# Loads of a batch held back until the convolution two batches earlier

## The chip, the core and the metric

The kernel runs on one core of one Trainium2 chip. The metric is the device time of one execution in microseconds (us). All times below are of that kind, or are read from the hardware profile of one execution.

## What is computed

The input x has 8 batches of 4224 rows with 192 columns, in float32. Two stages follow one another. Shortened from the reference:

```python
# stage 1: causal convolution along the rows, 7 taps, one softmaxed tap vector per head
w = softmax(weight)                       # 8 heads x 7 taps; a head is 24 of the 192 columns
y[b, s, h, :] = sum_k w[h, k] * x[b, s + k - 6, h, :]
# stage 2: mixing over the rows of a batch
W_tok = (y @ w_q) @ (y @ w_k).T / 8       # 4224 x 4224 per batch
out = relu(W_tok @ y) @ w_out
```

The kernel never forms W_tok. It uses that (y w_q)(y w_k)^T y is (y w_q) times the small matrix w_k^T (y^T y), so each batch needs the 192x192 Gram matrix y^T y, a 64x192 matrix made from it, and then row by row products.

## The kernel before

**Tiling.** A batch is cut into 35 chunks of 122 rows (NCC = 35). Each chunk is loaded with the 6 rows before it, so that one 128x128 band matrix per head does the convolution of a chunk as one matrix product. Loads go in groups of chunks: batch 0 has four groups (9, 9, 9 and 8 chunks), each later batch has two (18 and 17 chunks). The tile `XW` (line 355) has room for all 8 batches, so no load overwrites anything that is still read.

**Loads** (`gen_load`, lines 535 to 574). A load is issued by POOL with `e.dma_start` on line 565, and converts float32 to bfloat16 on its way. The first group of a batch is two DMAs (chunk 0, which lacks the 6 rows before it, and the other 17), the last group is two as well (16 chunks, and the short last one). That makes 34 DMAs. POOL does nothing else after the start apart from building the identity (line 426), and it issues the loads in the order of the batches. In the kernel before, a load of a later batch needs only the identity, the zeroed end of `XW`, or nothing: POOL may issue it at any time.

**Convolution** (`gen_conv`, lines 636 to 675). For each group there are four matrix operations, one per pair of heads (hp 0 to 3), each of four matmuls (lines 391 and 392) from `XW` and `BAND` into PSUM. An evacuation by ACT or DVE (line 671) writes `Y`, which has two buffers: batch b uses the buffer of batch b-2. Each of the four operations needs the load of its group.

**Later stages.** Of `Y` the kernel makes transposes (lines 691 and 726), the Gram matrix (line 787), the product with w_q (lines 751 and 755), the mixing (lines 878 and 890), a relu (lines 907 and 908) and the product with w_out (lines 935 and 953). The result goes through `out_sb`, four buffers, and out by DMAs that SP issues (line 978). The mixing of batch b runs beside the convolution, transposes and Gram matrix of batch b+1.

**Order.** Every operation is an `Op` with its engines, the operations that it needs, those that it only has to follow (`after`), and a priority `vt` taken from the list `TURNS` by the operation's number. `Planner.plan` (lines 143 to 213) places them one after another at planned times: an operation can be chosen once all that it needs or follows is placed, it is ready when what it needs has ended, and among the ready ones of an engine the lowest `vt` goes first. For a load, the planned landing is the later of its end plus 1500 ns and a fixed figure `lands` (line 573). `Program.place` (lines 232 to 274) then turns each need into a semaphore wait on the engine's own instruction stream, and leaves out those that an earlier wait covers. PE, ACT, DVE, POOL and SP each run their stream in that fixed order.

Of the kernel before, what the change touches and what calls it, by code (L numbers as in the profile page):

```python
# [279 lines left out]
def bass_lightweight_conv__then__hypermixer_token_mlp_kernel(  # L280
# [33 lines left out]
    def groups_of(b):  # L314
        size = 9 if b == 0 else 18
        return [list(range(c, min(c + size, NCC))) for c in range(0, NCC, size)]
# [60 lines left out]
    def add(*a, dma=None, kind=None, **k):  # L377
        op = Op(*a, **k)
        op.dma = dma
        op.kind = kind  # L380
        op.vt = TURNS[len(planner.ops)]
        return planner.add(op)

    def evac_ns(cols, fast=1):
        return {"ACT": 56 + cols / 1.2, "DVE": 62 + cols / (0.96 * fast)}
# [3 lines left out]
    def halves(e, out, lhsT, rhs, **k):  # L389

        e.matmul(out[0:64], lhsT[:, 0:64], rhs, **k)  # L391
        return e.matmul(out[64:128], lhsT[:, 64:128], rhs, **k)  # L392
# [137 lines left out]


    load = {}
    at = [5000.0]

    def gen_load(b, gi):
# [97 lines left out]
    def mm_ns(n, k=1):  # L633
        return k * (n / 2.4 + 2.5)

    def gen_conv(b, gi):
        cs = groups_of(b)[gi]
        n = len(cs)
        c0, yb = cs[0], b % 2
        pairs_in_bank = 2 * n * GRP <= 512  # L640
        nb = 1 if pairs_in_bank else 2
        gap = n * GRP if pairs_in_bank else 512
        for hp in range(H // 2):
            vt = b + c0 / NCC - 0.15 + 0.02 * hp

            def conv(e, op, hp=hp):
                last = None
                for i in range(2):
                    h = 2 * hp + i
                    o = op.bank * 512 + i * gap  # L650
                    last = halves(
                        e,
                        PS[:, o : o + n * GRP],
                        BAND[:, h, :],
                        XW[:, b, c0 : c0 + n, GRP * h : GRP * h + GRP],
                        start=True,
                        stop=True,
                    )
                return last

            ev_needs = [r for r in y_read.get((b - 2, "all"), [])]
            mm = add(
                "PE", conv, mm_ns(n * GRP, 2), needs=[*load[b, gi], *bands, zero_x, zero_x0], after=ev_needs, banks=nb, vt=vt, kind="conv")

            def evac(e, op, hp=hp, mm=mm):
                o = mm.bank * 512
                src = PS[0:CW, o : o + 2 * gap].rearrange("p (t n) -> p t n", t=2)[:, :, 0 : n * GRP]
                src = src.rearrange("p t (c g) -> p t c g", g=GRP)
                dst = Y[0:CW, yb, c0 : c0 + n, 2 * GRP * hp : 2 * GRP * hp + 2 * GRP]
                dst = dst.rearrange("p c (t g) -> p t c g", t=2)  # L670
                return e.copy(dst, src) if op.engine == "ACT" else e.tensor_copy(dst, src)  # L671

            ev = add(both, evac, evac_ns(2 * n * GRP), needs=ev_needs, drains=mm, vt=vt, kind="y")
            for c in cs:
                y_done.setdefault((b, c), []).append(ev)
# [312 lines left out]
    for b in range(B + 1):  # L988
        nxt = []
        if b < B:  # L990
            for gi in range(len(groups_of(b))):
                gen_conv(b, gi)
            for c in range(0, NCC, 8):
                gen_transpose(b, list(range(c, min(c + 8, NCC))))
            evqs = [gen_wq(b, j) for j in range(NSB)]
            grams = []
            step = 6
            for c in range(0, NCC, step):
                cs = list(range(c, min(c + step, NCC)))
                grams += gen_gram(  # L1000
                    b, cs, c == 0, c + step >= NCC, [g_read] if c == 0 and g_read else [], grams[:1]
                )
            evm = gen_mix_weights(b, grams)
            nxt = [(b, j, evm, evqs[j]) for j in range(NSB)]
        for job in later:
            gen_mix(*job)
        later = nxt

    planner.plan()

    program = Program(semaphore)
# [47 lines left out]
```

## Time and profile before

| What | Value |
|---|---|
| median of 3 runs | 177.17 us (176.81, 177.17, 178.93) |
| profiled execution, first to last instruction | 175.7 us, that is 1.5 us under the median |
| PE busy (matmul) | 157.1 us, 89% |
| ACT, DVE busy | 123.5 us, 118.0 us |
| POOL busy | 30.3 us, all of it in the first 53 us |
| bytes moved by the DMA engines | 40.36 MB, mean 230 GB/s |
| loads of x (queue q0) | 36128 packets, 13.61 MB as written |
| stores (most of queue q1) | 44 DMAs, 25.95 MB written to HBM |
| granted TensorE clock, mean | 0.990 |

The profile lists no separate run time for the profiled execution, so its span stands for it, and the 1.5 us are what a run has beyond the span, together with the scatter of the runs.

The page gives the busy time of each engine, then the span in 40 slices of 4.4 us with a digit for the busy share in tenths, then the DMA queues, then the chain of work that ended last. In that chain, "issue" is time in which an engine waited for nothing that the profile shows. Line numbers are those of the kernel.

### The profile page before, as it was taken

What the parts mean: (1) busy time and instruction counts of PE and PEld (TensorE: products, weight loads), DVE (VectorE), ACT (ScalarE), POOL (GpSimd) and SP (SyncE); (2) the same over time, 40 slices, a digit from 0 to 9 for tenths busy, and PEclk for the clock granted to TensorE, in tenths of its full rate; (3) what the DMA queues carried; (4) which work ended last, traced back from release to release, by engine and by line L of the source; (5) the groups of instructions that cost most, each with busy time, mean ns of one, the idle gap of its engine ahead of it and who ended that gap; (6) DMA issues with size and microseconds to landing.
All of it is one profiled execution on the core that took longest, in us unless ns stands there. A gap on an engine that the chain in (4) does not pass through costs nothing.

```text
span 175.7 us, 7099 instructions
## 1 busy us (share of the span) xinstructions
PE 157.1 (89%) x3226; PEld 121.7 (69%) x3226; DVE 118.0 (67%) x216; ACT 123.5 (70%) x206; POOL 30.3 (17%) x39
## 2 busy tenths in 40 slices
PE   0289799888999999899989979999999999999990
PEld 0179666776787787668778766878767777877550
DVE  6556587765766677586787738689688675765740
ACT  3243677597787948668648747888888896698980
POOL 7999452524230000000000000000000000000000
PEclk9999999999999999999999999999999999999995
DMA  3999999999999999999999999067283045987787
GB/s 30 162 189 186 205 191 193 191 196 277 193 279 194 286 309 268 343 250 243 304 264 282 237 194 348 24 244 297 103 343 127 4 175 216 356 347 309 265 303 262
DMA packets 48157, 40.36 MB, mean 230 GB/s; under 512 B 37632, under 2 KB 40960, under 8 KB 48128
## 3 DMA queue, kind: packets, MB, share of 16 engines
q0 software_dynamic: 36128, 13.61, 65.1%
q1 hardware_dynamic: 12000, 26.31, 40.9%
q8 instruction: 25, 0.41, 0.9%
q14 instruction: 4, 0.03, 0.1%
HBM read 27.56 MB, written 25.95 MB: 305 GB/s over the span
## 4 chain that ended last, share of the span: by engine, by line
PE 88%; issue 4%; DVE 3%; ACT 2%
PE ps L391 25%; PE ps L787 14%; PE ps L935 8%; PE ps L392 7%; PE ps L395 6%; PE ps L726 6%; PE ps L878 5%; PE ps L751 4%; PE ps L890 4%; PE ps L755 4%; PE ps L396 3%; ACT rt L907 1%; ACT out_sb L970 1%; DVE band L527 0%; DVE xw L416 0%
## 5 line engine op out<-in xcount | busy, mean ns | idle before, releaser
L970 ACT COPY out_sb<-ps 128x768 f32<-128x768 f32 (+1 forms) x46 | 34.7, 768 | 15.1 <-PE ps L392 11.3
L671 ACT CAST y<-ps 122x816 bf16<-122x816 f32 (+3 forms) x46 | 35.7, 791 | 13.2 <-PE ps L392 12.8
L907 ACT ACTIVATE rt<-ps 128x1024 bf16<-128x1024 f32 (+3 forms) x44 | 34.1, 800 | 6.4 <-PE ps L878 4.5
L787 PE MATMUL ps<-y 122*64 122x192 bf16 (+4 forms) x840 | 33.8, 222 | 2.2 <-issue 2.2
L970 DVE COPY out_sb<-ps 128x768 f32<-128x768 f32 (+1 forms) x26 | 21.6, 840 | 19.7 <-PE ps L392 18.5
L392 PE MATMUL ps<-wol,rt 128*64 128x192 bf16 x264 | 33.9, 255 | 1.0 <-issue 1.0
L787 PEld LDWEIGHTS ps<-y 122*64 122x64 bf16 (+1 forms) x840 | 31.1, 112 | 4.9 <-issue 2.8
L565 POOL DMA_DIRECT2D xw<-in_x_dram x34 | 29.9, 893 | 22.3 <-issue 21.5
L391 PE MATMUL ps<-wol,rt 128*64 128x192 bf16 x264 | 33.7, 255 | 0.0
L391 PE MATMUL ps<-xw,band 128*64 128x432 bf16 (+3 forms) x144 | 31.8, 335 | 1.5 <-DVE band L527 0.9
L392 PE MATMUL ps<-xw,band 128*64 128x432 bf16 (+3 forms) x144 | 32.1, 337 | 1.1 <-issue 1.1
L391 PEld LDWEIGHTS ps<-wol,rt 128*64 128x64 bf16 x264 | 24.1, 138 | 8.1 <-issue 2.0
L908 DVE TENSOR_SCALAR rt<-ps 128x512 bf16<-128x512 f32 (+3 forms) x36 | 23.6, 674 | 8.2 <-PE ps L878 7.6
L671 DVE CAST y<-ps 122x864 bf16<-122x864 f32 (+3 forms) x26 | 23.6, 912 | 8.0 <-PE ps L392 7.5
L698 DVE COPY ytl<-ps 128x976 bf16<-128x976 bf16 (+1 forms) x40 | 23.0, 591 | 3.9 <-PE ps L396 3.3
L392 PEld LDWEIGHTS ps<-wol,rt 128*64 128x64 bf16 x264 | 24.1, 138 | 1.2 <-issue 1.2
L396 PE MATMUL ps<-ident,y 122*64 122x122 bf16 x280 | 21.1, 219 | 0.0
L395 PE MATMUL ps<-ident,y 122*64 122x122 bf16 x280 | 21.0, 219 | 0.0
L935 PE MATMUL ps<-woh,rt 64*128 64x192 bf16 x264 | 20.4, 250 | 0.2 <-ACT rt L907 0.2
L395 PEld LDWEIGHTS ps<-ident,y 122*64 122x64 bf16 x280 | 18.1, 112 | 2.0 <-issue 0.5
L726 PE MATMUL ps<-ident,y 122*64 122x122 bf16 (+1 forms) x344 | 17.1, 220 | 1.3 <-DVE y L671 0.7
L396 PEld LDWEIGHTS ps<-ident,y 122*64 122x64 bf16 x280 | 17.7, 112 | 0.0
(95 smaller groups left out, 218.8 us busy)
## 6 DMA issues: line engine op xcount, KB each, us to landing
out_dram<-out_sb SPq DMA_DIRECT2D x28, 768.0 KB, 5.1
xw<-in_x_dram POOLq DMA_DIRECT2D x7, 816.0 KB, 33.2
xw<-in_x_dram POOLq DMA_DIRECT2D x7, 768.0 KB, 33.7
out_dram<-out_sb SPq DMA_DIRECT2D x8, 384.0 KB, 3.3
xw<-in_x_dram POOLq DMA_DIRECT2D x2, 432.0 KB, 8.3
out_dram<-out_sb SPq DMA_DIRECT2D x8, 96.0 KB, 4.3
xw<-in_x_dram POOLq DMA_DIRECT2D x1, 384.0 KB, 5.2
xw<-in_x_dram POOLq DMA_DIRECT2D x8, 45.8 KB, 25.0
```

The source lines that it names most:

```text
L391: e.matmul(out[0:64], lhsT[:, 0:64], rhs, **k)
L392: return e.matmul(out[64:128], lhsT[:, 64:128], rhs, **k)
L395: e.transpose(out[0:64], in_[:, 0:64], identity)
L396: return e.transpose(out[64:128], in_[:, 64:128], identity)
L565: lambda e, op, part=part: e.dma_start(*part),
L671: return e.copy(dst, src) if op.engine == "ACT" else e.tensor_copy(dst, src)
L726: last = e.transpose(ps[64 * i : 64 * i + HI, o : o + w], Y[0:w, yb, c, LO:D], IDENT[0:w, 0:w])
L787: mm = e.matmul(bank(GB)[p : p + 64, o : o + z - r], Y[0:w, yb, c, r : r + 64], Y[0:w, yb, c, r:z], start=st, stop=end, skip_group_check=True,
L907: return e.activation(dst, src(), AF.Relu)
L908: return e.tensor_scalar(dst, src(), 0.0, None, op0=ALU.max)
L935: last = e.matmul(bank(op.bank + a)[:, o : o + D], RT[64 * a : 64 * a + HI, slot, 2, i:n:nt], WOH[64 * a : 64 * a + HI, :], start=i == q, ...
L970: return e.copy(dst, src) if op.engine == "ACT" else e.tensor_copy(dst, src)
```

## The change

After all operations are made, and before the planner runs, every load of a batch from 2 on gets one more need: a convolution of the batch two before it. A batch from 3 on waits, group by group, for the same group of that batch. Batch 2 waits for groups 0 and 2 of the four groups of batch 0. `conv_of[b, gi]` is overwritten in the loop over the pairs of heads, so it holds the operation of hp 3, whose place in the planner's order need not be the last of the four.

```diff
     load = {}
+    conv_of = {}
     at = [5000.0]
...
-            mm = add(
+            mm = conv_of[b, gi] = add(
                 "PE", conv, mm_ns(n * GRP, 2), needs=[*load[b, gi], *bands, zero_x, zero_x0], after=ev_needs, banks=nb, vt=vt, kind="conv")
...
+    for (b, gi), ops in load.items():
+        if b >= 2:
+            for op in ops:
+                op.needs.append(conv_of[b - 2, gi if b > 2 else 2 * gi])
+
     planner.plan()
```

It touches 24 of the 34 load DMAs, and 12 groups. No operation is added or removed, and no transfer changes its size.

## The prediction, made before the changed kernel ran

> **What bounds the kernel now.** I read the page first (busy times, slices, chain), then the chain in order of time, then POOL's timeline and the DMA views.
>
> ```profile
> PE 157.1 (89%) x3226; PEld 121.7 (69%) x3226; DVE 118.0 (67%) x216; ACT 123.5 (70%) x206; POOL 30.3 (17%) x39
> ...
> PE   0289799888999999899989979999999999999990
> ...
> DMA  3999999999999999999999999067283045987787
> ...
> q0 software_dynamic: 36128, 13.61, 65.1%
> ...
> PE 88%; issue 4%; DVE 3%; ACT 2%
> ```
>
> PE is the bound: 88% of the chain that ended last is its own work. The DMA engines are full from the start to slice 25 (25 x 4.4 = 110 us), and then have room. The loads of x (q0) are what fills them: the trace's last q0 packet starts at 105.66 us. PE's dips (7, 8, 7) lie in the full part; from there to the last slice but one it is at 9 throughout. The stretches say the same:
>
> ```profile
> 92.00:106.00 14.00, 13.01 (x308) 10.77 (x303) 9.15 (x16) 9.03 (x16) 0.00 (x0) 1.00 1.26 244
> 106.00:116.00 10.00, 10.00 (x185) 7.16 (x183) 7.70 (x17) 8.67 (x13) 0.00 (x0) 1.00 0.38 147
> ```
>
> The first pair is the window and its length, the second PE's busy time and count, the last three the granted clock, the DMA share and GB/s. PE loses 1 us in 14 with the loads, nothing in 10 without, at the same clock of 1.00. What it loses there stands in the chain:
>
> ```profile
> 19.20 1.28 issue
> ...
> 32.64 0.50 issue
> ...
> 39.08 1.07 issue
> ...
> 70.06 0.90 issue
> ...
> 89.60 0.59 issue
> ...
> 102.10 0.99 issue
> ```
>
> Six pauses, 5.33 us, and no data is waited for in them. I counted PE's instructions (matmuls and weight loads together) up to each: 448, 960, 1216, 2496, 3264 and 3776, all 192 past a multiple of 256. The instruction queue of the DMA page (q8) has 25 packets of 16384 B, one about every 6 us, 0.9 to 1.0 us each, and each of the six pauses ends 1.4 to 1.5 us after one has landed. So they are waits for PE's next 256 instructions. Until 100.72 us, under the loads, 14 such fetches start, when PE is 43 to 120 instructions short of the block, and 6 come late. The 11 after 104 us start 134 to 264 short, and none is late. One loaded fetch costs 5.33 / 14 = 0.38 us on average.
>
> The Trainium skill, page "Runtime: NRT & Kernel Launch", section "Instruction fetch mechanics", has the same blocks of 16 KiB and 256 instructions, and says that the cost of crossing a block is mostly hidden. The trace agrees on the block and not on the cost, 5.33 us; by that page the third term below would be 0 and the sum 177.2.
>
> Last, POOL, whose issues the change touches:
>
> ```profile
> 2.63 16.51 POOL L565 DMA_DIRECT2D xw<-in_x_dram  x19
> 21.63 2.26 POOL L565 DMA_DIRECT2D xw<-in_x_dram  x3 [2.48 <-issue]
> ...
> 51.29 1.71 POOL L565 DMA_DIRECT2D xw<-in_x_dram  x2 [4.16 <-issue]
> ```
>
> And the landings of the same line (issue to landing):
>
> ```profile
> DMA to landing us min/median/max: 4.1/28.7/53.9
> ```
>
> POOL runs far ahead: 20 issues in the first 19 us, the last at 52.5, and up to 53.9 us pass until a landing. A load waits in its own queue, not for POOL. This decides the case: a load that is issued later loses nothing while an earlier load still keeps the queue busy.
>
> **The change part by part.** (1) The waits. 24 DMA instructions get a need and 12 of them become a wait on POOL. Behind them on POOL stand only later loads, and none of those is let go sooner than the one ahead of it. SP and its stores are not passed or held. PE, ACT and DVE get no instruction. POOL is idle from 53 us on, so the waits themselves cost 0. A load's two issues take about 1.8 us (1.2 and 0.6) and the first q0 packet starts 3.02 - 1.30 = 1.7 us after its issue began.
>
> (2) Landings. The release is the end of the head pair 3's matmuls (timeline of the convolution; in the planner's order of the kernel before, hp 3 stands first, third, fourth, fourth, second, second, second, second, last, last, second and sixth of eight for the twelve loads). "Queue" is when the preceding load landed, by the trace's semaphore records; "lands" is its time before; "needed" is its first convolution matmul. All us, first / second group.
>
> Batch 2: release 9.3 / 16.4, queue 25.6 / 30.3, lands 30.3 / 34.5, needed 34.4 / 37.8.
> Batch 3: release 25.6 / 30.9, queue 34.5 / 39.1, lands 39.1 / 45.5, needed 47.7 / 54.4.
> Batch 4: release 35.9 / 40.5, queue 45.5 / 51.0, lands 51.0 / 56.8, needed 67.9 / 73.5.
> Batch 5: release 48.7 / 57.3, queue 56.8 / 67.7, lands 67.7 / 77.1, needed 90.2 / 92.2.
> Batch 6: release 77.3 / 85.0, queue 77.1 / 84.1, lands 84.1 / 93.0, needed 105.7 / 119.2.
> Batch 7: release 91.4 / 95.8, queue 93.0 / 99.7, lands 99.7 / 106.0, needed 129.7 / 134.0.
>
> For batches 2 to 5 release + 1.8 lies before the queue's time (nearest: 48.7 + 1.8 = 50.5 against 56.8), so their packets move as before. Batch 6 is the only gap: its first packets come at 77.3 + 1.8 = 79.1, 2.0 us after the queue ran dry; the second group at 86.8 against 84.1 + 2.0 = 86.1, 0.7 more. Batch 7 is released before 95.7 and follows without a gap, so its last landing is 106.0 + 2.7 = 108.7. The least room for a convolution is 3.3 us, batch 2's second group, whose landing does not move; batch 6 keeps 105.7 - 86.1 = 19.6. Cost on PE's path: 0. If hp 3 were last everywhere, releases move by at most 4.1 us and the table ends the same.
>
> (3) Fetches. The loads now fill the DMA engines to 108.7 instead of 106.0. The fetch that started at 104.50 before would be a loaded one, and the next (109.46) perhaps. The 2 us gap at 77 to 79 meets no fetch (74.91 and 81.34, neither late), so it gains 0. One loaded fetch more: from 0 to 1.28 (the largest pause), two: to 2.56. I take the mean of a loaded fetch, 0.38. Downwards the end is -5.33, all six pauses gone, if their cause were the depth of the waiting queue; that is the first rival.
>
> (4) The plan. A load's planned landing is the later of its end plus 1.5 and the fixed `lands`. A convolution also has to follow all transposes and Gram products of the batch two before, which come after that batch's convolutions. So the new need can't be what a convolution waits for, and PE's order should stay: 0. If it moves, see the third rival.
>
> Sum, against the profiled execution: 175.7 + 0 + 0 + 0.4 + 0 = 176.1; with the 1.5 us to the median of the runs, 177.17 + 0.38 = 177.5.
>
> **Rivals.** *No change but noise or one or two pauses more* is the forecast: 176 to 179.7 (177.17 + 2.56), the three runs of before alone spreading from 176.81 to 178.93. This includes that the change hardly does what it says: ten of twelve loads wait in POOL for what they waited for in the queue. Chance 0.80.
>
> *Faster: a shorter queue lets fetches through.* If a fetch stands behind everything that POOL has issued, a short backlog ends the pauses: 177.17 - 5.33 = 171.8. For it: all six lie under the loads. Against it: four fetches from 44 to 63 us, with the backlog longest, were not late, and the one at 100.72, with only the last load left, was late by 0.99. Chance 0.06.
>
> *Slower: POOL's issue becomes the bound.* The loads are now written one by one while DVE and PE run, instead of far ahead. Let a load's issue take T. From 10.2 us on POOL writes one load per T, and batch 5's second half, the eighth, lands at about 10.2 + 8T + 2; it is late when this passes 92.2, so from T = 10.0 us on. At T = 10.6 PE would wait 4.8 us: 182. For it: nothing hides an issue any more. Against it: single issues took 0.55 to 1.34 us throughout, also from 21 to 53 us beside DVE's copies, so T is 1.8. Chance 0.06. The Trainium skill, page "SBUF — State Buffer", section "SBUF: two separate sides", warns of this: while DVE runs certain fast copies, GpSimd cannot write descriptors, and a transfer of 620 ns was seen to take 3100. By that factor of 5 T would be 9 us, just under the point, and the time some three loaded fetches more, 178.3; the durations of POOL's issues above do not show it.
>
> *The planner puts PE's work in another order.* PE has no idle time from 106 to 160 us, so another order can mostly only lose; a pause like the 2.0 us of ACT's relu in the chain at 162.97, twice, gives 181. Against it: (4). Chance 0.05. The remaining 0.03 is something I don't see, of either sign.
>
> **How the numbers follow.** The likeliest case gives 177.5. Its own range is 176 to 179.7; with the scatter of three runs below, 175.6 to 179.7 holds about 8 in 10, and what is left out are the rivals. About 2%, 173.6 and 180.7, is what a measurement of this kernel can tell from no change. Faster by over 2%: the first rival and a part of the unseen, 0.07. Slower: the second and most of the third, 0.11. Within: 0.82.
>
> **What would show it.** POOL's issues of x spread to about 97 us; the DMA row full to slice 25 as before, with a dent near 77 us at most; last landing near 109 us; no PE wait on a load of x in the waits; "issue" pauses of 4 to 7 us in the chain, all at block ends and none after 115 us; PE busy 157. It is wrong if PE waits for `xw`, if the issue rows of POOL grow beyond 3 us, if PE's operations stand in another order, or if the pauses vanish though the DMA row stays full.

## The result, and the profile after

The changed kernel takes 179.66 us (median of 20 runs, 178.82 to 181.74), the kernel before 177.74 us beside it (20 runs, 176.62 to 178.93). The ratio is 1.0114, with a 95% interval of 1.009 to 1.0137: slower by about 2 us, which is less than 2% and clear of noise. The forecast was 177.5 us and no change that can be measured; the time lies at the upper edge of its range, and the loss is real. The two profiled executions differ by as much: spans of 175.7 and 177.7 us.

The page of the changed kernel, with the lines that answer to those shown of before:

```profile
PE 157.0 (88%) x3226; PEld 121.1 (68%) x3226; DVE 118.0 (66%) x216; ACT 123.8 (70%) x206; POOL 30.4 (17%) x39
...
PE   0289599879989989799969999999999999999980
...
DMA  2999999999999999859999999648283045987686
...
q0 software_dynamic: 36128, 13.61, 65.0%
...
PE 80%; DMA 5%; DVE 4%; issue 4%; ACT 3%; DVEq 0%
```

No engine does more work than before, within 0.3 us. Two things are new late in the row of slices. The DMA row has a dent in its 17th and 18th slice (8, 5: 71 to 80 us), and PE a 6 in its 21st (89 to 93 us). And the chain that ended last now runs for 5% of the span through a DMA, where the page before names none. (The 5 in PE's fifth slice is the pause near 19 us, 1.87 us now and 1.28 before; the part on the fetches below comes back to it.)

POOL's timeline shows that the waits are there, and that batch 6 had to wait longest (the bracket is POOL's idle time and what ended it):

```profile
48.94 1.89 POOL L566 DMA_DIRECT2D xw<-in_x_dram  x2 [6.33 <-PE ps L392]
58.24 1.72 POOL L566 DMA_DIRECT2D xw<-in_x_dram  x2 [7.41 <-PE ps L392]
78.65 1.89 POOL L566 DMA_DIRECT2D xw<-in_x_dram  x2 [18.70 <-PE ps L392]
86.49 1.72 POOL L566 DMA_DIRECT2D xw<-in_x_dram  x2 [5.95 <-PE ps L891]
```

The DMA in the chain is one store, in the chain between 78 and 93 us:

```profile
79.76 1.50 ACT out_sb L971 x2
...
81.28 9.36 DMA out_dram<-out_sb
...
90.73 0.36 DVE out_sb L971
91.09 1.21 DVE wqt L772 x2
...
92.34 0.41 PE ps L891 x2
```

Read it downwards. ACT fills an output buffer, SP issues its store at 81.28, and the store lands 9.36 us later. DVE needs that buffer for its next copy into `out_sb`; behind the copy stand DVE's two `wqt` copies, and PE's mixing waits for those. The waits say what it cost. On DVE and then on PE:

```profile
DVE out_sb L971 <- DMA out_dram<-out_sb: 2.2, 1, 2.2
```

```profile
PE ps L891 <- DVE wqt L772: 0.9, 1, 0.9
PE ps L395 <- DVE out_sb L971: 0.8, 1, 0.8
```

PE lost 1.7 us there, in two pauses next to each other: its transposes (L395) went on with the end of DVE's copy, its mixing (L891) with the end of the `wqt` copies. Before, the same store was issued at 80.2 and landed at 87.4, after 7.2 us (store landings are worked out from the semaphore records of the trace), and DVE's copy ran at

```profile
87.49 0.36 DVE L970 COPY out_sb<-ps 128x192 f32<-128x192 f32 x1
```

without any wait, 0.1 us after the landing. The kernel before had that little room, and nothing on its page shows it, because a wait that just fails to happen leaves no line. Its list of waits did have a hint, a wait of ACT for another output buffer, near 66 us, with no pause of PE behind it:

```profile
ACT out_sb L970 <- DMA out_dram<-out_sb: 2.4, 1, 2.4
```

Why the store was late stands in the stretches. First before, then after; the last three columns are the granted clock, the DMA share and GB/s:

```profile
76.00:80.00 4.00, 4.00 (x78) 2.82 (x72) 3.36 (x7) 3.27 (x5) 0.00 (x0) 1.00 1.36 278
80.00:84.00 4.00, 4.00 (x96) 3.29 (x93) 1.97 (x4) 3.30 (x8) 0.00 (x0) 1.00 1.51 215
```

```profile
76.67:79.91 3.24, 3.24 (x62) 2.22 (x61) 2.79 (x6) 2.51 (x4) 1.19 (x2) 1.00 0.55 205
79.91:85.77 5.86, 5.86 (x135) 4.86 (x133) 3.25 (x5) 5.14 (x10) 0.63 (x1) 1.00 1.01 98
```

In the trace's packet records the load queue q0 is empty from 76.67 to 79.91 us, 3.24 us. Then batch 6's load restarts, and slowly: its packets move 42, 26, 109 and 157 GB/s in the four microseconds from 80, against about 190 when q0 runs alone in the kernel before (82 to 84 us). The first two figures belong to its small DMA (chunk 0, 46 KB) and to the step to its large one, whose first packet comes at 81.27, as good as together with the store's issue at 81.28. The store is issued into that. Its first packet moves at 85.77, 4.5 us after the issue (before: 83.92, 3.7 us, of which the stores ahead of it moved until 81.6), and in the 5.86 us from the restart to that packet the core moves 98 GB/s in all. The store's shares on the 16 DMA engines then end far apart: the first at 88.9, the last at 90.6 (before: 86.6 and 87.4).

### The profile page after: what moved, and what is told of

The parts are those of the page before. It is cut to its first block, busy times and chain, and to the rows that moved or that the text cites. A ratio compares the mean times of both kernels' runs of the same rounds, so it can differ in the third digit from the quotient of the medians.

```text
span 177.7 us, 7099 instructions
## 1 busy us (share of the span) xinstructions
PE 157.0 (88%) x3226; PEld 121.1 (68%) x3226; DVE 118.0 (66%) x216; ACT 123.8 (70%) x206; POOL 30.4 (17%) x39
## 4 chain that ended last, share of the span: by engine, by line
PE 80%; DMA 5%; DVE 4%; issue 4%; ACT 3%; DVEq 0%
PE ps L391 23%; PE ps L788 13%; PE ps L936 8%; PE ps L392 6%; PE ps L727 6%; PE ps L395 5%; DMA out_dram<-out_sb 5%; PE ps L879 5%; PE ps L752 4%; PE ps L891 4%; PE ps L756 4%; PE ps L396 3%; ACT out_sb L971 2%; ACT rt L908 1%; DVE wqt L772 1%
## 5 line engine op out<-in xcount | busy, mean ns | idle before, releaser
L788 PE MATMUL ps<-y 122*64 122x64 bf16 (+4 forms) x840 | 33.7, 222 | 2.8 <-issue 2.8
L395 PE MATMUL ps<-ident,y 122*64 122x122 bf16 x280 | 20.8, 217 | 0.8 <-DVE out_sb L971 0.8
L395 PEld LDWEIGHTS ps<-ident,y 122*64 122x64 bf16 x280 | 17.7, 110 | 3.0 <-DVE out_sb L971 1.0
L734 DVE COPY yth<-ps 128x512 bf16<-128x512 bf16 (+1 forms) x40 | 14.4, 375 | 4.6 <-PE ps L727 4.5
```

Of the source, the lines that this page charges most:

```text
L395: e.transpose(out[0:64], in_[:, 0:64], identity)
L788: mm = e.matmul(bank(GB)[p : p + 64, o : o + z - r], Y[0:w, yb, c, r : r + 64], Y[0:w, yb, c, r:z], start=st, stop=end, skip_group_check=True,
```

## The experiments

Each was compared with the kernel before on the same chip, by 6 to 12 timed runs but for `e12_late2b`, and has one profile, of one of these runs. All keep the planner's order (in the profiles ACT, DVE and SP have the same instructions in the same order in every kernel, POOL too but for the cut loads of `e8_pieces`). Where some waits are taken away, the loads behind the last kept wait follow it directly.

**Which waits cost: four variants.**

`e1_g25`, batches 2 to 5 wait, 6 and 7 follow batch 5:

```diff
-                op.needs.append(conv_of[b - 2, gi if b > 2 else 2 * gi])
+                op.needs.append(conv_of[3, 1] if b > 5 else conv_of[b - 2, gi if b > 2 else 2 * gi])
```

> The waits of batches 2 to 5 stay, those of batches 6 and 7 go: their loads follow directly behind batch 5's second half (release near 57 us), so the load queue never runs dry. Theory D (dry queue): the loss comes from the 3 us in which the load queue is empty before batch 6; a load that restarts then meets the stores, a store lands 2 us later than usual, and PE waits 1.7 us for it. D expects no such store wait, PE pauses at block ends of 5 to 6.5 us, and a time within +0.5 us of the kernel before (ratio 0.998 to 1.004). Theory J (just in time): each held load by itself costs some 1.9 / 12 = 0.16 us, by later instruction fetches; J expects 8 x 0.16 = +1.3 us (ratio 1.007). In the changed kernel's one profile two new pauses of 0.5 us stood near 52 and 65 us; J wants them here too, D doesn't care.

`e2_g67`, only batches 6 and 7 wait:

```diff
-        if b >= 2:
+        if b >= 6:
```

> Only batches 6 and 7 wait (releases near 77, 85, 91 and 96 us); batches 2 to 5 are issued as early as before. D expects the empty stretch near 77 to 80 us, a store of 9 us or more behind it, DVE or ACT waiting 2 us on it, and +1.5 to +2 us (ratio 1.008 to 1.011). J expects 4 x 0.16 = +0.6 us (ratio 1.004).

`e3_g6a`, one release is left, batch 6's first:

```diff
-        if b >= 2:
+        if b >= 6:
...
-                op.needs.append(conv_of[b - 2, gi if b > 2 else 2 * gi])
+                op.needs.append(conv_of[4, 0])
```

> A single wait is left, that of batch 6's first half; batch 6's second half and batch 7 follow it at once. D expects the same empty stretch and store wait as with all waits, and nearly the whole loss, +1.3 to +2 us (ratio 1.007 to 1.011). J expects +0.2 us (ratio 1.001).

`e4_nodry`, all wait, batch 6 for head pair 0 (`conv_of` now kept by head pair):

```diff
-                op.needs.append(conv_of[b - 2, gi if b > 2 else 2 * gi])
+                op.needs.append(conv_of[b - 2, gi if b > 2 else 2 * gi, 0 if b == 6 else 3])
```

> All twelve waits stay, but batch 6 waits for head pair 0 of the same convolutions, which runs first, so its loads are released near 69 and 75 us, before the queue runs dry at 77. D expects no empty stretch, no store wait of PE, and a time within +0.5 us of the kernel before (ratio up to 1.003), against +1.9 with head pair 3. J expects the full +1.9 us (ratio 1.011), as all twelve loads are still held.

| Kernel | median us | ratio (95%) | load queue empty before batch 6 | store of 81 us |
|---|---|---|---|---|
| e1_g25 | 178.34 | 1.0044 (1.0019 to 1.007) | no | 7.2 us, no wait |
| e2_g67 | 179.06 | 1.0081 (1.0047 to 1.0115) | 6.37 us | 9.4 us, DVE waits 2.2 |
| e3_g6a | 179.54 | 1.0107 (1.0061 to 1.0152) | 2.47 us | 9.5 us, DVE waits 2.3 |
| e4_nodry | 178.28 | 1.0023 (0.9995 to 1.0052) | no | 7.2 us, no wait |

One wait out of twelve, that of batch 6's first half, makes nearly the whole loss, and letting batch 6's two waits go sooner (POOL issues the loads at 69.3 and 74.9 us instead of 78.7 and 86.5), with all others kept, takes most of it back. The profile of `e3_g6a` has the same line as the changed kernel:

```profile
90.53 0.36 DVE L971 COPY out_sb<-ps 128x192 f32<-128x192 f32 x1 [2.27 <-DMA out_dram<-out_sb]
```

Theory J, an equal price for each held load, wanted 1.001 for `e3_g6a` and 1.011 for `e4_nodry`: it fails on both. But `e1_g25`, at 1.0044, lies between D's 1.004 and J's 1.007; see the rest below.

**The way to PE: one more output buffer.** `e6_nout5` is the whole change, `e7_nout5_before` the kernel before (the changed one with `b >= 20`, so that no load waits), both with

```diff
-    NOUT = 4
+    NOUT = 5
```

> The whole change, with five output buffers instead of four; the order of all instructions stays. A copy then needs the store of five blocks back and not of four. D1 and D2 both say that the loss reaches PE only through the output buffer: the late store stays late (9 us), nobody waits for it, and the ratio falls from 1.011 to 0.998 to 1.004. If the loss had another way to PE (fetches, or the convolution), it would stay at 1.008 or more.

> The kernel before with five output buffers, as the control. In the kernel before no pause of PE comes from an output buffer (one wait of ACT of 2.4 us near 66 us, with no PE pause behind it), so 0 by all theories: ratio 0.998 to 1.002.

Measured: 178.12 us, 1.0029 (1.0008 to 1.0049), and for the control 177.54 us, 0.9998 (0.9976 to 1.002). With five buffers the store is as late as ever (issued 81.0, landed 90.4, 9.3 us; the queue is empty for 2.85 us), and DVE copies without waiting:

```profile
88.25 0.35 DVE L971 COPY out_sb<-ps 128x192 f32<-128x192 f32 x1
```

So three quarters of the loss, 1.0114 down to 1.0029, go through the output buffer, and the fifth buffer gives nothing where no store is late. This shows the path for that part of the loss.

**The empty queue, or when it restarts.** Theory D so far left open whether any dry stretch costs (D1) or only a restart at the wrong time (D2). Four kernels move the release of batch 6, all other waits kept, with `conv_of` by head pair as in `e4_nodry`.

`e5_late2` and, for another look at it, `e12_late2b`:

```diff
-                op.needs.append(conv_of[b - 2, gi if b > 2 else 2 * gi])
+                op.needs.append(conv_of[4, 1, 2 + gi] if b == 6 else conv_of[b - 2, gi if b > 2 else 2 * gi, 3])
```

> All waits stay, but batch 6 is released later still, by head pairs 2 and 3 of batch 4's second group (near 81 and 86 us instead of 78 and 86). The load queue is then empty longer, from 77 to about 83 us, and restarts after the store of 81 us has been issued, not 1.4 us before its issue. Theory D1 (any dry stretch costs): +1.9 us or more (ratio 1.011 and up). Theory D2 (the restart costs only where it falls just ahead of a store, whose buffer is needed back within 7 us): the store of 81 us lands in 3.5 to 6 us, no DVE wait on it, ratio 1.000 to 1.004; a restart just ahead of the next store (near 85 us) could cost something instead. Batch 6's first half lands near 92 us, needed at 107.

> The kernel of e5_late2 once more, for a second profile: six of its seven timed runs were at 179.1 to 179.8 us and one at 177.7, and its one profile (span 175.8) had no wait for an output buffer. If the loss of the six has the same cause as in the changed kernel, a profile of a slow one shows the store of 81 us landing 9 us after its issue, or that of 84.5 us 10 us after it, and DVE or ACT waiting 2 us for its buffer near 90 us. If it shows no such wait at a span of 177 us or more, that cause is not the whole of it.

`e9_late6`, `e10_r401` and `e11_r411`, where `at` is (4, 1, 3), (4, 0, 1) and (4, 1, 1):

```diff
-                op.needs.append(conv_of[b - 2, gi if b > 2 else 2 * gi])
+                op.needs.append(conv_of[at] if (b, gi) == (6, 0) else conv_of[b - 2, gi if b > 2 else 2 * gi, 3])
```

> All waits stay; both halves of batch 6 wait for the last convolution of batch 4 (near 86 us). The load queue is empty from 77 to about 88 us, the longest dry stretch of all, and restarts after the stores of 81 and 84.5 us have landed on an otherwise idle queue (4 to 5 us each). D1 (any dry stretch costs): ratio 1.010 or more. D2 (only a restart just ahead of a store whose buffer is due soon): no output buffer is waited for by DVE near 90 us, and the ratio is 0.998 to 1.004; the stores issued near 88 us meet the restart, but their buffers are due only near 105 us and later.

> All waits stay; batch 6's first half is released by head pair 1 instead of 3, the operation just ahead of it (0.8 us sooner). The queue is dry for about 2 us instead of 3, and the bulk of the load starts about 2.2 us ahead of the store of 81 us instead of 1.4. D2: the load is more nearly up to speed when the store comes, which lands sooner by some 0.5 us; ratio 1.005 to 1.009. D1: a shorter dry stretch, in proportion 1.007.

> All waits stay; batch 6's first half is released by head pair 1 of batch 4's second group (near 76 us, 2.5 us sooner than in the changed kernel). The queue is dry for 0.5 to 1 us at most. D1 and D2 both expect nearly no loss, ratio 1.000 to 1.004, no DVE wait on an output buffer near 90 us.

| Kernel | median us | ratio (95%) | queue empty (profile) | store of 81 us |
|---|---|---|---|---|
| after | 179.66 | 1.0114 (1.009 to 1.0137) | 76.7 to 79.9 | 9.4 us, DVE waits 2.2 |
| e10_r401 | 179.98 | 1.0104 (1.0063 to 1.0145) | 76.5 to 78.5, 0.7 again at 79.2 | 8.9 us, DVE waits 1.7 |
| e11_r411 | 178.48 | 1.0037 (1.0004 to 1.007) | 75.0 to 78.3 | 7.2 us, no wait |
| e9_late6 | 178.25 | 1.0034 (1.0001 to 1.0066) | 77.4 to 87.4 | 3.4 us, no wait |
| e5_late2 | 179.51 | 1.0098 (1.0068 to 1.0128) | 76.5 to 81.0, 2.3 more at 81.6 | 4.3 us, no wait |
| e12_late2b | 180.15 (one run) | | 76.8 to 81.6, 2.4 more at 82.2 | 4.8 us, no wait |

D1 falls: 10 us without loads cost `e9_late6` about 0.3%, 2.5 us cost `e3_g6a` 1.1%, and `e11_r411` has the same 3.24 us as the changed kernel, 1.6 us sooner, and two thirds less loss. (That its queue would be empty for 1 us at most, as expected, was wrong.) In `e9_late6` the store of 81 us has the DMA engines to itself, and the copy that needs its buffer runs at once:

```profile
87.96 0.35 DVE L971 COPY out_sb<-ps 128x192 f32<-128x192 f32 x1
```

The profile of `e9_late6` is of the fastest of its 12 runs, which go from 177.45 to 180.82 us; what the longer ones waited for was not seen.

In `e11_r411` the load has run for 3 us when the store comes and moves 153 GB/s; the store lands at 88.6 us, and the copy runs at 88.64, with no more room than in the kernel before. Its timed runs spread from 176.85 to 180.19 us, as one would expect at such an edge; that the spread comes from there is an inference.

`e10_r401` missed its forecast of 1.005 to 1.009, though the store landed 0.5 us sooner as forecast (8.9 us). The expectations above reckon the load's lead from the restart's first packet, 1.4 us ahead of the store in the changed kernel. What puts these profiles in order is the first packet of the large load: 0.01 to 0.05 us ahead of the store's issue in the changed kernel, `e2_g67`, `e3_g6a` and `e6_nout5` (store 9.3 to 9.5 us), 0.9 us in `e10_r401` (8.9 us), 2.1 us in `e11_r411` (7.2 us).

`e5_late2` went against D2, which wanted at most 1.004. Its only profile had a span of 175.8 us and no wait for a buffer, and is not of the kind of the six runs near 179.5. The second profile, with a span of 178.3 us, has no wait for a buffer near 90 us either, so by the expectation above the late store is not the whole cause. It shows another one:

```profile
88.28 0.22 PE ps L752 x2
89.36 0.50 PE ps L788 x12
90.46 0.22 PE ps L891 x2
90.67 1.84 issue
92.52 0.34 PE ps L391
```

That is the chain from 88 to 94 us. The pause falls on PE's instruction 3264, a block end, and the packet with that block's instructions starts at 90.25 us and takes 0.88 us; the one before it started at 79.52. In the kernel before the same block's packet started at 87.76 and the pause was 0.59 us. Here the bulk of batch 6's load came up from 84.6 us on (73, 106, 111, 129 GB/s in the microseconds from 85). The store of 84.7 us took 9.7 us, without a waiter, and the fetch came too late. So what meets the restart may be something else than a store, and the loss depends on who needs it, and when. This rests on one profile, in which the pauses at block ends account for 1.1 us of the 2.6 us by which its span exceeds that of the kernel before. The profile of `e5_late2` itself speaks against a fixed rule: the same restart, at 83.9 us, and a store of 84.1 us that took 9.7 us, but the block's packet started at 88.25 and the pause was 0.52 us. That the six slower runs of `e5_late2` had the long pause was not seen, so their loss stays open.

**The rest of 0.2 to 0.4%.** Five kernels in which PE does not wait for a store (e1, e4, e6, e9, e11) still stand at 1.002 to 1.004; the interval of e4 reaches below 1. `e13_w00`, `e14_h31` and `e15_h7`:

```diff
 e13:  op.needs.append(conv_of[0, 0])
 e14:  if b >= 6:  ...  op.needs.append(conv_of[3, 1])
 e15:  if b >= 7:  ...  op.needs.append(conv_of[b - 2, gi])
```

> All loads of batches 2 to 7 wait, but for the first convolution of batch 0, which ends at 9.3 us, before POOL gets to them (10.2 us). The waits are there and delay nothing. Open is a rest of 0.2 to 0.4% that four kernels without a store wait on PE still show. If the rest comes from loads that are issued late, this kernel has none: ratio 0.998 to 1.002. If it came from the waits as instructions, it would stay at 1.003.

> Only batches 6 and 7 wait, and both for the last release of batch 5 (near 57 us), so the queue never runs dry and nothing is delayed in landing. If the rest comes from late issue of any loads, there is a part of it here: ratio 1.001 to 1.004, with the pause at PE's block 2240 (65 us), which is in all profiles with waits so far and in none of three without. If late issue matters only while the early batches are loaded: 1.000 and no pause at 65 us.

> Only batch 7 waits (release near 91 and 95 us, at which time the queue still works on batch 6). By theory D2 the store wait near 90 us is gone, ratio 1.000 to 1.004; the load queue may have short gaps near 92 to 100 us, behind which no buffer is due within 10 us. Of the rest this is the late end: about 1.001 if it grows with the number of loads held, as much as the others (1.003) if it is a matter of the last fetches.

Measured: 177.55 us, 0.9994 (0.9975 to 1.0014); 177.51 us, 1.0004 (0.9988 to 1.002); 177.38 us, 0.999 (0.9961 to 1.0019). The wait instructions cost nothing, nor does holding batch 7, nor late issue of batch 6 while the queue is still full. The only group left that all five have in common is the held batches 2 to 5, alone in `e1_g25`: 1.0044. How they cost it is not settled, nor that they do: `e8_pieces` below holds no load and stands at 1.0035, and the runs of e9 and e11 spread over 3 us, so that their 0.3% need not be the same loss in every run. I had a pause at 65 us in mind (PE's block 2240), but it is in the profile of `e13_w00` too (0.23 us), which has no loss.

**A try at a faster kernel.** `e8_pieces` cuts the loads of the kernel before (the line that issues them; where `cuts` is made is left out):

```diff
-                lambda e, op, part=part: e.dma_start(*part),
+                lambda e, op, cuts=cuts: [(e.dma_start(*c), 16) for c in cuts],
```

> The kernel before, without waits, each load of 16 or 17 chunks from batch 1 on cut into DMAs of at most 5 chunks (14 of them become 56, the last of each 1 or 2 chunks). A try at a faster kernel: PE's pauses at block ends (5.3 us in all) come from instruction fetches that are late while the load queue is full. If a fetch has to wait until a DMA engine has worked off its share of one load DMA (136 row packets an engine, now 40), the fetches come earlier, the pauses fall to 1 to 3 us and the ratio to 0.985 to 0.993. If the turn of a queue is a fixed run of packets, nothing changes: ratio 0.998 to 1.003. POOL's issue time per half batch grows from 1.8 to about 3 us, which the queue's backlog hides.

Measured: 178.12 us, 1.0035 (1.0013 to 1.0057), no faster. PE's pauses at block ends sum to 6.5 us in its profile, against 5.3, and its store of 81 us lands after 7.2 us as before. How long a fetch or a store stands behind the loads does not go with the size of one load DMA. The Trainium skill, page "DMA: Bandwidth & Descriptors", section "Queues, rings and completion order", says that each DMA engine takes turns between the queues that have work and drains one whole packet of descriptors before it turns to the next. With `e8_pieces` that agrees as far as it goes; what makes up such a packet, no run here shows. By that rule the size of one load DMA would change nothing; that a store is later still behind a restart is not in it.

No version here beats the kernel before.

## Why the prediction was wrong, point by point

*The bound and PE's pauses* were read rightly: PE stays the bound, and the pauses at block ends sum to 5.3 us in the profile after as before. (The instruction counts 448 to 3776 come out of the trace if PE's semaphore instructions are counted too, and not matmuls and weight loads alone.) The sum stood on 177.17 us, the median of three runs; twenty runs gave 177.74.

*(1) The waits.* That they cost nothing on POOL is shown by `e13_w00` (0.9994). The sentence "SP and its stores are not passed or held" is the step that failed. It looked at the issue queues, where it holds, and not at the DMA engines, which loads and stores share. The stores were put at 0 without a reason; in their place the runs showed one store that landed after 9.36 us instead of 7.21, a wait of DVE of 2.2 us for its buffer, and 1.7 us lost by PE, of which a fifth buffer takes nearly all back. The prediction had quoted the landing times of the loads and not one of a store. The row was there: four output buffers, most stores landing 7 to 10 us after their issue under the loads, and one buffer landing 0.1 us before its next use. A cost of 0 for the stores needed a margin beside it, as the convolutions had theirs.

*(2) The landings.* Batches 2 to 5 kept their queue as forecast. A gap before batch 6 was forecast as the only one, with 2.0 us. Measured were 3.24 us between packets. From the landing before it, by which the forecast reckoned, it is 2.7 us (77.17 to 79.91), because PE was 1 us later by then. That no convolution waits for `xw` was right. The duration of batch 6's first half was not: I moved its end by the gap alone, to 86.1 us, and it landed at 93.26, 13 us after its restart instead of 7; in that time the two stores of 81.3 and 84.7 us moved too. The last load landed at 115.1 us instead of 108.7.

*(3) The fetches* were priced at +0.38 us, and the sum of the pauses in the pair of profiles moved by nothing: two near 52 and 65 us came, the one near 19 us grew by 0.6 us, two near 90 and 102 us went. The timed rest of 0.2 to 0.4% is of the size of that term, yet it does not come from the late end of the loads, to which the term was tied: `e1_g25` has it with its last load packet at 105.6 us as before, and `e15_h7` doesn't, with its last load landing at 110.4 us.

*(4) The plan* did not move: no order of instructions changed.

*The rivals.* The faster one is out: with a much shorter backlog the pauses stayed. POOL's issue did not become a bound: two DMAs took 1.7 to 1.9 us throughout, so of the lock that the Trainium skill, page "SBUF — State Buffer", section "SBUF: two separate sides", warns of nothing is seen here; whether DVE's copies in this kernel are of the kind that takes it, no run here shows. The case that happened, a store that is late for its buffer, was not among the rivals. The range held it, by the width that I gave to noise and fetches.

## What to carry to other kernels

A transfer that is moved in time has two sets of neighbours: those behind it in its own queue, and everything else that uses the same DMA engines then. For each store in flight compare its landing with the next use of its buffer; a margin of 0.1 us shows on no page as a wait, and it is the first thing to break. When loads are held back, either keep their queue from running dry, or let it restart where nothing in flight is due soon, or give the output one more buffer: here each of the three took back most of the loss.

## What the runs showed of the hardware

The load queue, once empty, restarted slowly: 42, 26, 109 and 157 GB/s in successive microseconds, with the step from a small load to a large one in the second, and it was not back at the 190 of the kernel before when the store's packets began 5.9 us after the restart. A store issued together with the large load's first packet waited 4.5 us for its own first packet, against 3.9 when the large load had run for 0.9 us (`e10_r401`), 3.2 when it had run for 2.1 us (`e11_r411`), 3.7 in the kernel before, where the loads never stop, and 0.9 on engines free of loads (`e9_late6`). Its landing was spread over 1.8 us between the DMA engines instead of 0.8. That the engines have come out of step in the restart is an inference from that spread; it wasn't tried apart, and `e11_r411` has the same spread of 1.8 us with a store that landed after 7.2 us.
